# The order of the first loads and the place of the last copies in a gated linear attention with a mixture of attention experts

## Chip, cores and metric

The kernel runs on one core of a Trainium2 chip. The metric is the device time of one execution in microseconds (us), less is better. Three runs of the kernel before gave 327.18 us in the median (326.1 to 327.74).

## What is computed

Two stages. The first is a recurrence per batch and head with a decay rate for each row of the state; its output is the input of the second, attention with four experts, of which two are weighted per token.

```python
# q, k, v, alpha: (4, 8, 768, 48); alpha in 0.8 to 1
for t in range(S):
    state = alpha[:, :, t, :, None] * state + einsum('bhd,bhe->bhde', k[:, :, t], v[:, :, t])
    y[:, :, t] = einsum('bhd,bhde->bhe', q[:, :, t], state)
x = y.transpose(0, 2, 1, 3).reshape(B, S, 384)
logits = x @ w_gate                      # 4 experts, the best 2 weighted by softmax
for e in range(4):
    q, k, v = x @ wq[e], x @ wk[e], x @ wv[e]          # 64 wide
    a = softmax(causal(scale * q @ k.T))
    out += weight[e] * (a @ v @ wo[e])
```

## The kernel before

The recurrence is cut into 24 chunks of 128 steps (6 per batch). For each chunk VectorE makes running products of the decay rates with scans (`prep_r`, `prep_c`, line 181) and multiplies queries and keys by them (`prep_kq`, line 201). TensorE then transposes the keys (`gla_t`, line 237), forms the state's update (`gla_u`, line 266), the scores within the chunk (`gla_a`, line 220) and the output (`gla_y`, line 305). Three chunks are a unit; for each of the 8 units the attention with experts follows (projections, scores, softmax, transposes, products, and `outp`, line 499, into a result tile that is copied out of PSUM by `outp_o` and written by `store`). Products that need more than one rounded factor use a high and a low part; the low part of the value weights is made on TensorE by subtraction with a negated identity, `nid` (lines 730 and 731), after ScalarE has rounded the high part (line 747).

A planner in the kernel, run when the program is built, sets the order. Each step is an `op` with its dependencies, engines and an assumed length; `run` places them one by one. The opening is written by hand: `opening` (line 901) issues the first loads, calls `constants` (line 149) and then tells the planner with `came` when each load is taken to arrive. At most eight loads are outstanding: each load waits for the landing of the one eight places before it.

In the opening SyncE's queue issues chunk 0's first half of rates and of queries and keys, then rates and queries and keys of chunk 1, values of chunk 0, value weights, rates and queries and keys of chunk 2, and so on. Chunk 0 comes in two halves. Its second half is issued by ScalarE, after a table load, a small activation on `ones` (line 151) and the copy into `nid` (line 160). TensorE meanwhile runs warming matmuls on constants (line 896).

A range check on the scans ends in one integer, `cnt`. Every engine loads it into a register (`good`, line 960) and branches on it (line 967); if it is 0, the recurrence is computed again step by step. At the end of the last unit the third result tile is copied in two halves, by ScalarE and by VectorE, each stored on its own queue (lines 712 to 719); `good` depends on these two stores.

Of the kernel before, what the change touches and what calls it, by code (L numbers as in the profile page):

```python
# [12 lines left out]
AF = mybir.ActivationFunctionType  # L13
# [4 lines left out]
B, H, S, D = 4, 8, 768, 48  # L18
DM = H * D
# [4 lines left out]
NU = B * NC // HALF  # L24
NG = B * NC
NT = S // 128
P = 112
# [9 lines left out]
    P="t.0 u.0 a.0 wx.v.0 a.1 t.1 wx.v.1 y.0 u.1",  # L37
    V="r.0.0 c.0.0 r.0.1 c.0.1 kq.0.0 kq.0.1 r.1.0 c.1.0 kq.1.0 r.2.0 m.1.1 m.1.0 S.1 c.2.0 kq.2.0 xl.0 sa.1 kt.2 xl.1 kr.2 m.2.1 m.2.0 r.3.0 c.3.0",
    A="kr.0 kt.0 wvh m.0.1 m.0.0 wl.v.0 kt.1 kr.1 B.1 wl.v.1 wqh.0 xh.0 xh.1 B.2 vo.0.0 wqh.1 xh.2 kt.3 vo.0.1 ph.0.0.0 ph.0.0.1 woh ck.0 vo.0.2 ck.2 kr.3 B.3",
    G="e.0.0 e.0.1 e.1.0 m.0.1 m.0.0")  # L40
# [23 lines left out]
def tile_gla_moe(ctx: ExitStack, tc: tile.TileContext, qk_d, al_d, v_d, wqk_d, wv_d, wo_d, nat_d, vn_d, out_d):  # L64
    nc = tc.nc
    V, A, G, PE, SY = nc.vector, nc.scalar, nc.gpsimd, nc.tensor, nc.sync
# [5 lines left out]
    def fixed(name, shape, dt=F32):  # L72
        return consts.tile(shape, dt, name=name)
# [11 lines left out]
    def at(name):  # L85
        pool, i = where[name]
        return unit[pool][i]
# [4 lines left out]
    def view(x, *shape):  # L92
        n = "abcd"[:len(shape)]
        return x.rearrange(f"p ({' '.join(n)}) -> p {' '.join(n)}", **dict(zip(n[:-1], shape[:-1])))
# [5 lines left out]
    wo = view(raw[2][:, 780:780 + 2 * DM], 2, DM)  # L100
# [4 lines left out]
    def pieces(n):  # L105
        return [(0, 2), (2, 4)] if n == 0 else [(0, tiles(n))]
# [4 lines left out]
    def al(n, i=0):  # L111
        p0, p1 = pieces(n)[i]
        x = rates(n, i).rearrange("p (i z) -> p i z", i=2)
        return x[:, :, 0:(p1 - p0) * CW].rearrange("p i (a w) -> p i a w", w=CW)

    def load_al(n, i, eng):
        p0, p1 = pieces(n)[i]
        eng.dma_start(al(n, i), al_d[n, :, :, p0:p1])

    def load_q(n, i, eng):  # L120
        p0, p1 = pieces(n)[i]
        eng.dma_start(at(("T", n))[:, p0:p1, 0:2 * C], qk_d[n, :, p0:p1])

    def load_v(n):
        SY.dma_start(at(("v", n)).rearrange("s p e -> s (p e)"), v_d[n // NC, n % NC])
# [3 lines left out]
    ident = fixed("ident", [128, 128])  # L129
# [9 lines left out]
    ones = fixed("ones", [128, 1])  # L139
# [7 lines left out]
    nid = fixed("nid", [128, 128], F32R)  # L147

    def constants():
        G.memset(ones, 1.0)  # L150
        A.activation(ones, ones, AF.Copy)
        G.memset(d1r, TINY)
        G.memset(d1r[:, :, 0:1], 1.0)
        for t in d1c:
            V.memset(t, TINY)
        G.memset(mask, 1.0)
        G.affine_select(mask, mask, [[1, C]], OP.is_ge, 0.0, base=-(C - 1), channel_multiplier=1)
        G.memset(ident, 0.0)
        G.affine_select(ident, ident, [[1, 128]], OP.not_equal, 1.0, base=0, channel_multiplier=-1)
        A.activation(nid, ident, AF.Copy, scale=-1.0)  # L160
        for t in ST:
            G.memset(t, 0.0)
        for t in unit["kt"]:
            G.memset(t.rearrange("t p (s d) -> t p s d", s=2)[:, :, :, D:64], 0.0)
        G.memset(acc, 0.0)
        for t in SM:
            G.memset(t, 0.0)
        for t in [t for i, t in enumerate(unit["T"]) if i not in WHOLE]:
            for r in (32, 96):
                G.memset(t[r:r + 32, 3], 0.0)  # L170
        G.memset(cmask, 0.0)
        G.affine_select(cmask[:, 384:512], cmask[:, 384:512], [[-1, 128]], OP.is_ge, -1.0e30, base=0, channel_multiplier=1)
        G.memset(lm, 0.0)
        G.affine_select(lm, lm, [[1, NE], [-1, NE]], OP.is_gt, SMALL, base=0, channel_multiplier=0)
# [64 lines left out]
    def copy(eng, out, src):  # L239
        if eng == "A":  # L240
            A.activation(out, src, AF.Copy)  # L241
        else:
            V.tensor_copy(out, src)  # L243
# [255 lines left out]
                PE.matmul(po[:, 0:DM], y[:, h, 128 * i:128 * i + 128], w[:, pair, :], start=(m == 0), stop=(m == 5))  # L499
                m += 1  # L500

    def outp_o(eng, u, i, c0=0, c1=DM):
        copy(eng, at(("ot", u, i))[:, c0:c1], at(("po", u, i))[:, c0:c1])

    def store(eng, u, i, c0=0, c1=DM):
        t0 = 128 * (3 * (u % 2) + i)
        eng.dma_start(out_d[u // 2, t0:t0 + 128, c0:c1], at(("ot", u, i))[:, c0:c1])

    ops, users = [], {}
    KB = dict(La=396, Lq=393, Lv=262, cp=98, st=196)  # L510
# [1 line left out]
    def op(key, target, deps, alts, uses=(), take=(), mode="", land=0.0, lock=False):  # L512
        o = dict(key=key, target=target, deps=list(deps), alts=alts, uses=list(uses), take=list(take), mode=mode, land=land, lock=lock)
        ops.append(o)
        for n in o["uses"]:
            users[n] = users.get(n, 0) + 1
        return o

    def dv(n):
        return 0.15 + 0.00105 * n  # L520

    def da(n):
        return 0.19 + 0.00081 * n

    def either(f, n, *a):
        return [("A", da(n), lambda: f("A", *a)), ("V", dv(n), lambda: f("V", *a))]
# [178 lines left out]
    def out_ops(u):  # L705
        tail, seq, step, base = plan(u)
        for i in range(3):
            z = (base + step * 6 + OFF["w"] + 0.1 * i) * PACE
            op(("w", u, i), z, [("ol", u, 0, 0, 3), ("ol", u, 1, i, i + 1) if tail else ("ol", u, 1, 0, 3)],
               [("P", 1.06, lambda i=i: outp(u, i))], [("yy", u, 0), ("yy", u, 1)], [("po", u, i)], "f")  # L710
            po, ot = ("po", u, i), ("ot", u, i)
            if tail and i == 2:
                for x, E, Q in ((0, "A", A), (1, "V", SY)):
                    c = (192 * x, 192 * x + 192)
                    op(("wo", u, i, x), z, [("w", u, i)], [alt for alt in either(outp_o, 192, u, i, *c) if alt[0] == E], [po, ot],
                       [] if x else [ot])
                    op(("st", u, i, x), z, [("wo", u, i, x)], [("S" if x else "A", 0.4, lambda Q=Q, c=c: store(Q, u, i, *c))], [ot],
                       land=2.2)
                continue
            op(("wo", u, i), z, [("w", u, i)], either(outp_o, DM, u, i)[:1 if tail and i else 2], [po, ot], [ot])  # L720
            op(("st", u, i), z, [("wo", u, i)], [("S", 0.57, lambda i=i: store(SY, u, i))], [ot], land=2.2)

    def both(low, w, high):
        f = lambda E: E.tensor_tensor(low, w, high.bitcast(F32), OP.subtract)
# [176 lines left out]
    def opening():  # L901
        arrive, z = {}, [LEAD]

        def came(key, kb):
            z[0] += kb / RATE
            arrive[key] = (z[0], "S")

        for n in range(4):
            where["T", n] = ("T", n)
        for n in range(3):  # L910
            where["v", n] = ("v", n)
        where["al", 0] = ("at", 0)
        plain = list(range(UNITS["al"]))
        for n in range(1, 4):
            where["al", n] = ("a", (2 * n - 2, 2 * n - 1)) if n in WHOLE else ("al", plain.pop(0))
        where["at", "wqk"], where["at", "wvo"] = ("at", 1), ("at", 2)
        load_al(0, 0, SY)
        load_q(0, 0, SY)
        constants()
        load_al(0, 1, A)  # L920
        load_q(0, 1, A)
        for key, kb in (("La", 0, 0), 264), (("Lq", 0, 0), 262), (("La", 0, 1), 264), (("Lq", 0, 1), 262):
            came(key, kb)
        z[0] += 0.5
        for n in (1, 2):
            load_al(n, 0, SY)
            load_q(n, 0, SY)
            load_v(n - 1)
            came(("La", n, 0), 132 * tiles(n))
            came(("Lq", n, 0), 131 * tiles(n))  # L930
            came(("Lv", n - 1), 262)
            if n == 1:
                SY.dma_start(wv, wv_d)
                came(("Lw", 1), 400)
        SY.dma_start(wqk, wqk_d)
        came(("Lw", 0), 786)
        load_v(2)
        came(("Lv", 2), 262)
        load_al(3, 0, SY)
        load_q(3, 0, SY)  # L940
        came(("La", 3, 0), 396)
        came(("Lq", 3, 0), 393)
        SY.dma_start(wo, wo_d)
        came(("Lw", 2), 393)
        warm(7, 32)
        return arrive, z[0]

    okm = fixed("okm", [128, NG + 1])
    cnt = fixed("cnt", [1, 1], I32)
# [5 lines left out]
    z = (NG + 4) * PACE  # L955
# [1 line left out]
    op(("pk",), z, [("ok",)], [("P", 0.05, lambda: PE.matmul(at(("pk",))[0:1, 0:1], okm[:, 0:1], ones, start=True, stop=True))],  # L957
       [], [("pk",)], "f")
    op(("cnt",), z, [("pk",)], [("V", 0.15, lambda: V.tensor_scalar(cnt, at(("pk",))[0:1, 0:1], 128.0 * NG, None, op0=OP.is_ge))], [("pk",)])
    op(("good",), z, [("cnt",), ("st", NU - 1, 2, 0), ("st", NU - 1, 2, 1)], [("P", 0.05, lambda: good.append(nc.values_load(cnt, min_val=0, max_val=1)))])  # L960
    good = []

    with tc.manual_schedule():
# [3 lines left out]
    with tc.If(good[0] == 0):  # L967
# [7 lines left out]
        st, kv, tm = (unit["a"][i][:, 0:12 * D].rearrange("p (a d) -> p a d", a=12) for i in (2, 3, 4))  # L975
# [30 lines left out]
        for u in range(NU):  # L1006
# [3 lines left out]
            for i in range(3):  # L1010
                t0 = 128 * (3 * hf + i)
# [94 lines left out]
```

## Time and profile before

| | us |
|---|---|
| median of 3 runs | 327.18 (326.1 to 327.74) |
| profiled execution | 326.7 |
| its span (first to last instruction) | 325.0 |
| TensorE busy | 313.2 |
| VectorE busy | 249.3 |
| ScalarE busy | 208.9 |
| GpSimd busy | 128.5 |
| mean granted clock of TensorE, as a share of full | 0.984 |

The profile shows one execution. Times in it count from the span's first instruction. PE is TensorE, DVE VectorE, ACT ScalarE, POOL GpSimd, SP SyncE; a q behind a name is the engine's sequencer, where DMAs are issued, registers loaded and branches taken. In the timeline a row gives start, length, engine, line, operation, output and input, count, and in brackets how long the engine had been idle and what ended that.

### The profile page before, as it was taken

To read this page: it belongs to the slowest core of one execution; us is meant where nothing else is said; L and a number is where in the kernel's file an instruction comes from. 1 tells how busy PE (TensorE), PEld (TensorE's weight loads), DVE (VectorE), ACT (ScalarE), POOL (GpSimd) and SP (SyncE) were. 2 spreads that over 40 slices of the span, in tenths; PEclk is the share of its full clock that TensorE was granted. 3 is DMA by queue.
4 is the path that set the end of the run, shared out by engine and by line. 5 is a ranking of instruction groups with operands and counts; after the bars stand their busy time and mean duration, and the time that the engine had idled before them with its cause. 6 is when DMAs were issued, how large, how long until landed. Compare 5 with 4: busy or idle time off the path is not lost.

```text
span 325.0 us, 11059 instructions
## 1 busy us (share of the span) xinstructions
PE 313.2 (96%) x4416; PEld 267.7 (82%) x4416; DVE 249.3 (77%) x679; ACT 208.9 (64%) x588; POOL 128.5 (40%) x197
## 2 busy tenths in 40 slices
PE   7299999999999999999999999999999999999995
PEld 2178998988997997998997997898897997888693
DVE  3569988999899998999799998766875745487620
ACT  2136598778776784757957775656873766377841
POOL 6014514553546257507507037405171344023510
PEclk9579999999999999999999999999999999999999
DMA  7993437464253335624352524302200000102001
GB/s 207 391 359 115 108 84 256 137 183 133 78 169 93 113 92 151 174 93 141 91 189 76 151 63 131 98 35 84 87 4 2 0 5 16 59 1 75 2 29 59
DMA packets 27037, 35.21 MB, mean 108 GB/s; under 512 B 2304, under 2 KB 23008, under 8 KB 26976
## 3 DMA queue, kind: packets, MB, share of 16 engines
q1 hardware_dynamic: 26288, 33.78, 34.1%
q8 instruction: 37, 0.61, 0.8%
q10 hardware_dynamic: 688, 0.62, 0.6%
q14 instruction: 24, 0.20, 0.2%
HBM read 27.61 MB, written 4.72 MB: 99 GB/s over the span
## 4 chain that ended last, share of the span: by engine, by line
PE 94%; DMA 3%; issue 1%; ACT 0%; POOL 0%; POOLq 0%
PE g L328 16%; PE g L455 12%; PE g L480 12%; PE g L305 11%; PE g L403 11%; PE g L354 8%; PE g L499 8%; PE g L220 7%; PE g L896 4%; DMA at<-in_al_dram 3%; PE g L237 2%; PE g L266 2%; PE g L730 0%; ACT ms L228 0%; PE g L731 0%
## 5 line engine op out<-in xcount | busy, mean ns | idle before, releaser
L440 POOL TENSOR_SCALAR a<-a,cf,gw 128x128 f32<-128x128 f32 (+5 forms) x96 | 81.7, 864 | 71.1 <-DVE cf L434 45.3
L428 ACT ACTIVATE a<-a,mx 128x256 f32<-128x256 f32 (+3 forms) x96 | 51.6, 540 | 8.9 <-DVE mx L417 8.8
L455 PE MATMUL g<-ident,a 128*128 128x128 f32 x336 | 53.8, 277 | 0.0
L328 PE MATMUL g<-x,wqkh 128*128 128x384 f32 x192 | 51.7, 350 | 0.0
L455 PEld LDWEIGHTS g<-ident,a 128*128 128x128 f32 x336 | 39.7, 140 | 5.8 <-issue 2.3
L232 POOL TENSOR_SCALAR_AFFINE_SELECT ms<-ms 128x512 f32<-128x512 f32 x31 | 21.3, 700 | 57.9 <-ACT ms L228 56.0
L243 DVE COPY at<-g 128x512 f32<-128x512 f32 (+3 forms) x62 | 29.2, 480 | 16.8 <-PE g L455 15.8
L480 PE MATMUL g<-at,vg 128*32 128x384 f32 (+2 forms) x648 | 39.7, 389 | 0.0
L403 PE MATMUL g<-k,q 64*128 64x256 f32 (+3 forms) x384 | 39.2, 336 | 0.0
L241 ACT ACTIVATE at<-g 128x512 f32<-128x512 f32 (+3 forms) x66 | 30.4, 466 | 8.3 <-PE g L455 6.5
L480 PEld LDWEIGHTS g<-at,vg 128*32 128x32 f32 x648 | 19.2, 110 | 18.6 <-issue 15.3
L305 PE MATMUL g<-ms,v 128*32 128x128 f32 x768 | 33.1, 274 | 0.0
L328 PEld LDWEIGHTS g<-x,wqkh 128*128 128x128 f32 x192 | 33.0, 189 | 0.0
L403 PEld LDWEIGHTS g<-k,q 64*128 64x128 f32 x384 | 28.6, 185 | 5.2 <-issue 2.3
L328 PE MATMUL g<-x,wqkl 128*128 128x384 f32 x96 | 32.3, 337 | 0.0
L354 PE MATMUL g<-wvh,x 128*128 128x260 f32 x144 | 31.7, 296 | 0.0
L417 DVE CUSTOM_DVE_ANT_0 a<-g,cmask 128x128 f32<-128x128 f32 (+2 forms) x64 | 28.2, 483 | 2.0 <-PE g L403 1.8
L499 PE MATMUL g<-woh,yy 128*128 128x384 f32 x96 | 28.1, 351 | 0.0
L220 PE MATMUL g<-T 48*128 48x128 f32 x384 | 26.4, 280 | 0.0
L220 PEld LDWEIGHTS g<-T 48*128 48x128 f32 x384 | 24.7, 193 | 1.4 <-issue 0.7
L228 ACT ACTIVATE ms<-g 128x512 f32<-128x512 f32 x31 | 17.3, 592 | 11.4 <-PE g L220 11.3
L354 PEld LDWEIGHTS g<-wvh,x 128*128 128x128 f32 x144 | 24.0, 190 | 0.4 <-ACT ms L228 0.4
(113 smaller groups left out, 629.1 us busy)
## 6 DMA issues: line engine op xcount, KB each, us to landing
al<-in_al_dram SPq DMA_DIRECT2D x21, 387.0 KB, 4.0
T<-in_qk_dram SPq DMA_DIRECT2D x21, 384.0 KB, 4.1
v<-in_v_dram SPq DMA_DIRECT2D x24, 256.0 KB, 4.1
out_dram<-ot SPq DMA_DIRECT2D x23, 192.0 KB, 2.3
T<-T SPq DMA_DIRECT2D x42, 48.2 KB, 2.2
a<-in_al_dram SPq DMA_DIRECT2D x2, 516.0 KB, 6.8
T<-in_qk_dram SPq DMA_DIRECT2D x2, 512.0 KB, 7.7
at<-in_wqk_dram SPq DMA_DIRECT2D x1, 768.0 KB, 8.6
```

The lines of the kernel that those rows point to most:

```text
L220: PE.matmul(pa[s][:, C * p:C * p + C], t[r:r + D, p, C:2 * C], t[r:r + D, p, 0:C], start=True, stop=True, tile_position=(r, 0))
L241: A.activation(out, src, AF.Copy)
L243: V.tensor_copy(out, src)
L305: PE.matmul(o[32 * j:32 * j + 32, k], l, r, start=(i == 0), stop=(i == len(parts) - 1), tile_position=(0, 32 * j))
L328: PE.matmul(pj[:, :W3], w[:, kt, cs], x[:, kt, :], start=(i == 0), stop=(i == 8))
L354: PE.matmul(pv[:, 0:260], x[:, kt, 128 * i:128 * i + 128], w[:, kt, :], start=(m == 0), stop=(m == 8))
L403: PE.matmul(sc(u, pair, i, e, x, c1 - c0), q[r, i0, ts], k[r, i1, c0:c1], start=(y == 0), stop=(y == 2), tile_position=(64 * e, 0))
L428: A.activation(a[:, c0:c1], src, AF.Exp, bias=mx[:, 1:2], scale=-1.0 if last else 1.0, accum_out=sm[:, x:x + 1])
L440: G.tensor_scalar(a[:, 0:n], a[:, 0:n], CF[u % 2][:, 3 * pair + i, e:e + 1], gw[:, u, i, eg:eg + 1], op0=OP.mult, op1=OP.mult)
L455: PE.transpose(pt[:, 128 * (j - j0):128 * (j - j0) + 128], a[:, 128 * j:128 * j + 128], ident)
L480: PE.matmul(o[r:r + 32, lo:n1], v[:, j % 3, 64 * eg + x:64 * eg + x + 32], at(("at", u, pair, e))[:, min(j, 4), at_off(j) + lo:at_off(j) + ...
L499: PE.matmul(po[:, 0:DM], y[:, h, 128 * i:128 * i + 128], w[:, pair, :], start=(m == 0), stop=(m == 5))
```

## The change

Chunk 0's two halves of rates go out first, both on SyncE's queue. Its two halves of queries and keys go out on ScalarE's queue, right behind the activation on `ones`. The copy into `nid` comes after them. The planner is told the new order of arrival and 0.2 us less for it. At the end, `good` no longer depends on the last stores but on the last product, and the copies of the last two result tiles depend on `good`; the last tile is copied whole by ScalarE and stored on its queue.

```diff
     def constants():
-        G.memset(ones, 1.0)
-        A.activation(ones, ones, AF.Copy)
         G.memset(d1r, TINY)
...
-        A.activation(nid, ident, AF.Copy, scale=-1.0)
...
-            if tail and i == 2:
-                for x, E, Q in ((0, "A", A), (1, "V", SY)):
-                    c = (192 * x, 192 * x + 192)
...
-            op(("wo", u, i), z, [("w", u, i)], either(outp_o, DM, u, i)[:1 if tail and i else 2], [po, ot], [ot])
-            op(("st", u, i), z, [("wo", u, i)], [("S", 0.57, lambda i=i: store(SY, u, i))], [ot], land=2.2)
+            late = tail and i > 0
+            op(("wo", u, i), z, [("w", u, i)] + [("good",)] * late, either(outp_o, DM, u, i)[:1 if late else 2], [po, ot], [ot])
+            op(("st", u, i), z, [("wo", u, i)], [("A", 0.4, lambda i=i: store(A, u, i)) if tail and i == 2 else
+                                                ("S", 0.57, lambda i=i: store(SY, u, i))], [ot], land=2.2)
...
-        load_al(0, 0, SY)
-        load_q(0, 0, SY)
+        for i in (0, 1):
+            load_al(0, i, SY)
+        G.memset(ones, 1.0)
+        A.activation(ones, ones, AF.Copy)
+        for i in (0, 1):
+            load_q(0, i, A)
         constants()
-        load_al(0, 1, A)
-        load_q(0, 1, A)
-        for key, kb in (("La", 0, 0), 264), (("Lq", 0, 0), 262), (("La", 0, 1), 264), (("Lq", 0, 1), 262):
+        A.activation(nid, ident, AF.Copy, scale=-1.0)
+        for key, kb in (("La", 0, 0), 264), (("La", 0, 1), 264), (("Lq", 0, 0), 262), (("Lq", 0, 1), 262):
             came(key, kb)
-        z[0] += 0.5
+        z[0] += 0.3
...
-    op(("good",), z, [("cnt",), ("st", NU - 1, 2, 0), ("st", NU - 1, 2, 1)], [("P", 0.05, lambda: good.append(nc.values_load(cnt, min_val=0, max_val=1)))])
+    op(("good",), z, [("cnt",), ("w", NU - 1, 2)], [("P", 0.05, lambda: good.append(nc.values_load(cnt, min_val=0, max_val=1)))])
```

Between these places the order of the instructions is the same on all five engines. The opening on ScalarE before (`at_63` holds the rates of chunk 0, `T_85` its queries and keys; `kt` are transposed keys):

```order
L151 ACT_TABLE_LOAD
L151 ACTIVATE ones<-ones 128x1
L160 ACTIVATE nid<-ident 128x128
L118 DMA at_63<-in_al_dram 128x2x258
L122 DMA T_85<-in_qk_dram 128x2x256
L241 ACTIVATE kt_69<-g_101 128x3x2x16
L241 ACTIVATE kt_69<-g_101 128x6x48
```

and now:

```order
L911 ACT_TABLE_LOAD
L911 ACTIVATE ones<-ones 128x1
L122 DMA T_85<-in_qk_dram 128x2x256 x2
L915 ACTIVATE nid<-ident 128x128
L238 ACTIVATE kt_69<-g_101 128x3x2x16
L238 ACTIVATE kt_69<-g_101 128x6x48
```

Both loads of queries and keys now stand ahead of the copy into `nid`, and the rates are gone from this queue. The opening on SyncE's queue now (`a` and `T_86` are rates, and queries and keys, of chunk 1, `v_92` values of chunk 0, `at_65` the value weights; the second `a` and `T_87` belong to chunk 2):

```order
L118 DMA at_63<-in_al_dram 128x2x258 x2
L118 DMA a<-in_al_dram 128x2x516
L122 DMA T_86<-in_qk_dram 128x4x256
L125 DMA v_92<-in_v_dram 128x512
L927 DMA at_65<-in_wvg_dram 128x780
L118 DMA a<-in_al_dram 128x2x516
L122 DMA T_87<-in_qk_dram 128x4x256
L125 DMA v_93<-in_v_dram 128x512
```

Before, the second place held `T_85<-in_qk_dram 128x2x256`; the rest is as it was. The end on ScalarE before (`ot` are result tiles, `yy` the products' operands):

```order
L486 ACTIVATE yy_81<-g_108 128x128
L486 ACTIVATE yy_81<-g_102 128x128
L241 ACTIVATE ot_96<-g_107 128x384
L241 ACTIVATE ot_97<-g_104 128x192
L507 DMA out_dram<-ot_97 128x192
L960 TENSOR_LOAD cnt
L967 COMPARE_AND_BRANCH
```

and now:

```order
L483 ACTIVATE yy_81<-g_108 128x128
L483 ACTIVATE yy_81<-g_102 128x128
L954 TENSOR_LOAD cnt
L238 ACTIVATE ot_96<-g_107 128x384
L238 ACTIVATE ot_97<-g_104 128x384
L504 DMA out_dram<-ot_97 128x384
L961 COMPARE_AND_BRANCH
```

The answer's load stands ahead of the last two copies, and the branch directly behind the last store. On SyncE the load likewise stands ahead of its last store, which is now that of `ot_96`.

## Rows read from the trace of the kernel before

**Rows 1.** The page: shares of the chain that ended last.
```profile
PE 94%; DMA 3%; issue 1%; ACT 0%; POOL 0%; POOLq 0%
```

**Rows 2.** Timeline of ScalarE, 0 to 32.
```profile
2.10 0.20 ACT L151 ACTIVATE ones<-ones 128x1 f32<-128x1 f32 x1
...
4.09 0.64 ACTq L118 DMA_DIRECT2D at<-in_al_dram  x1
4.77 0.86 ACTq L122 DMA_DIRECT2D T<-in_qk_dram  x1
```

**Rows 3.** Timeline of SyncE's queue, 0 to 32.
```profile
3.48 0.62 SPq L125 DMA_DIRECT2D v<-in_v_dram  x1
4.14 0.43 SPq L933 DMA_DIRECT2D at<-in_wvg_dram  x1
4.61 0.69 SPq L118 DMA_DIRECT2D a<-in_al_dram  x1
```

**Rows 4.** DMA issues, 0 to 9: count, KB each, us from issue to landing.
```profile
at<-in_wvg_dram SPq DMA_DIRECT2D x1, 390.0 KB, 6.9
T<-in_qk_dram ACTq DMA_DIRECT2D x1, 256.0 KB, 9.0
v<-in_v_dram SPq DMA_DIRECT2D x1, 256.0 KB, 6.1
a<-in_al_dram SPq DMA_DIRECT2D x1, 516.0 KB, 8.5
```

**Rows 5.** DMA queues, 7 to 8, then 9.5 to 10: packets, MB; q1 SyncE's, q10 ScalarE's.
```profile
q1 hardware_dynamic: 339, 0.37, 108.3%
...
q1 hardware_dynamic: 54, 0.13, 68.2%
q10 hardware_dynamic: 54, 0.06, 32.2%
```

**Rows 6.** Timeline of VectorE, 0 to 32.
```profile
12.06 0.70 DVE L181 TENSOR_TENSOR_SCAN at<-at,d1r 128x258 f32<-128x258 f32 x1 [6.26 <-DMA at<-in_al_dram]
...
13.60 1.27 DVE L201 TENSOR_TENSOR T<-T,at 128x512 f32<-128x512 f32 x2
...
18.67 1.23 DVE L181 TENSOR_TENSOR_SCAN a<-a,d1r 128x516 f32<-128x516 f32 x1
...
22.63 1.29 DVE L224 TENSOR_TENSOR ms<-g,mask 128x512 f32<-128x512 f32 x2 [2.51 <-PE g L220]
```

**Rows 7.** Timeline of TensorE at 14, and the chain's piece at 21.
```profile
14.37 1.03 PE L237 MATMUL g<-ident,T 128*128 128x128 f32 x3 [6.83 <-issue]
...
21.39 1.09 PE g L220 x16
```

**Rows 8.** Two stretches: busy time of five engines, granted clock, DMA share, GB/s.
```profile
8.00:10.00 2.00, 0.00 (x0) 0.00 (x0) 0.00 (x0) 0.00 (x0) 0.00 (x0) 0.89 1.05 400
18.00:20.00 2.00, 2.00 (x33) 1.82 (x24) 1.97 (x3) 0.00 (x0) 0.00 (x0) 0.55 1.08 387
```

**Rows 9.** The end: timelines of ScalarE and SyncE, then lines 960 and 967.
```profile
317.31 0.49 ACT L241 ACTIVATE ot<-g 128x384 f32<-128x384 f32 x1 [1.22 <-PE g L499]
318.37 0.33 ACT L241 ACTIVATE ot<-g 128x192 f32<-128x192 f32 x1 [0.56 <-PE g L499]
...
317.83 1.62 SPq L507 DMA_DIRECT2D out_dram<-ot  x2
...
L960 ACTq TENSOR_LOAD <-cnt x1: 487/487/487, 319.1 to 319.1; - x1
...
L967 SPq EVENT_SEMAPHORE  x8: 17/17/17, 323.0 to 323.6; - x8
...
L967 ACTq COMPARE_BRANCH  x1: 62/62/62, 319.7 to 319.7; - x1
L967 SPq COMPARE_BRANCH  x1: 50/50/50, 320.4 to 320.4; - x1
...
L967 ACTq EVENT_SEMAPHORE  x1: 17/17/17, 322.4 to 322.4; - x1
```

## What the change does to the time, from these rows

> **What bounds the kernel now.** The first view is the chain that ended last: TensorE holds 94% of it [rows 1]. The order of its instructions is fixed, so whatever lets it begin its first real work earlier moves everything behind it, as long as nothing else is late on the way. Two stretches are not TensorE's: the opening and the end.
>
> The second view is the opening, engine by engine. ScalarE finishes its table load and its little activation at 2.30, but the DMA of chunk 0's second half of rates goes out at 4.09 and that of its queries and keys at 4.77 [rows 2]. These queries and keys land 9.0 us after their issue, at 13.8 [rows 2, 4]. The rates of that half are what VectorE waits 6.26 us for, until 12.06; its two products of chunk 0 run from 13.60 to 14.87 [rows 6]. TensorE, out of its warming matmuls at 7.54, starts the transposes of chunk 0 at 14.37 after 6.83 us of nothing [rows 7]. Its granted clock went to the lower of its two levels (1.2 instead of 2.4 GHz) on the way: 0.89 is the mean of 8 to 10, so it fell at about 9.56, two us after the last matmul, and with a mean of 0.55 over 18 to 20 it came back at 19.8 [rows 8]. So 4.4 us of TensorE's work behind the transposes (15.40 to 19.8) ran at half speed.
>
> The third view is the end. After TensorE's last product, two copies of half a tile run one after the other, each with its store on another queue; then SyncE reads the answer of the range check, branches at 320.4, and its first instruction behind the branch runs at 323.0. ScalarE branches at 319.7 and goes on at 322.4 [rows 9].
>
> **What the change does to the opening.** On SyncE's queue the second half of the rates takes the place of the first half of the queries and keys, same size within 2 KB; the queue issues as many loads ahead of chunk 1 as before. So that half should land where the replaced load did, before 5.8, when VectorE's first half ends: VectorE was idle for 6.26 us up to 12.06, from 5.80 on [rows 6]. A half (scan, reciprocal, scan) takes 13.60 - 12.06 = 1.54, so both halves are scanned by 7.34 and the 6.26 us wait is gone.
>
> Next in line are the queries and keys, now both on ScalarE's queue, with no wait ahead of them, from 2.3 to about 3.8 (0.64 and 0.86 each [rows 2]). The second one decides. No row shows a load on this queue so early, so I bound it. *Early*: it has landed by 7.34 and costs nothing. *Late*: as slow as the same load was before, 9.0 us from its issue at 3.0, so 12.0. Between them I go by bytes, since loads issued one after another landed in that order. The value load of chunk 0 was the last of 258 + 256 + 516 + 512 + 256 = 1,798 KB and landed at 3.48 + 6.1 = 9.6 [rows 3, 4]. Ahead of and with the second queries load there will be 258 x 2 + 516 + 256 + 512 + 256 = 2,056 KB. But the two queues share packet by packet once both have work: 54 packets of each in half a us [rows 5]. Its 256 rows of 1 KB are then through when half of the 512 KB of SyncE's neighbour is: 1,800 KB, **9.6**. I take that; without the sharing it is 256 KB later, 0.7 us by the 375 GB/s of 7 to 8 (0.37 MB [rows 5]), 10.3.
>
> What speaks against more: before, ScalarE's transfers, issued at 4.09, had moved nothing by 8.0; between 7 and 8 only SyncE's queue shows packets [rows 5]. A second queue did not pass what had been issued ahead of it.
>
> The Trainium skill says as much of this edit (DMA: Bandwidth & Descriptors, "Issuing engines are not separate DMA queues"): loads issued by several engines run on the same DMA engines, and a second issuer saves issue time alone. By that rule the second load lands at 10.3 and the sum below is 0.7 us smaller, 320.1; rows 5 agree with it up to 8 us and not on the sharing after that.
>
> From 9.6 VectorE needs half of 1.27 us, so the products end at 10.2 instead of 14.87: VectorE is **4.6 us** earlier. TensorE's transposes ended 0.53 us behind (15.40), and from there to the end of the scores of chunk 1 (21.39 + 1.09 = 22.48) its chain ran 7.08 us without a wait [rows 7]. At the old clock it ends at 10.8 + 7.1 = 17.9, 4.6 earlier. At the full clock the 4.4 us shrink to 2.2, and it ends near 15.6, 6.9 earlier. Which? TensorE still stops at 7.54, now for some 2.7 us with two transposes in between, not for 6.8. The clock fell after two us of rest, so it may fall, but it comes back sooner. I take the middle, **5.8 us**.
>
> What covers this, and how thinly: VectorE begins the rates of chunk 2 at 18.67 - 4.6 = 14.1. They landed at 4.61 + 8.5 = 13.1 [rows 3, 4] and have the same bytes ahead of them now; 1.4 us later VectorE can take the masks it took at 22.63 [rows 6], so it caps the gain at about 7.1. The value weights landed at 4.14 + 6.9 = 11.0 and now have 514 KB more ahead, so about 12.4; ScalarE's rounding and TensorE's difference of them come at 13.5 to 14. If they land a us later, TensorE loses that us. The identity's negated copy moves behind two issues, to about 4; its first user, the subtraction of the rounded value weights, comes no sooner than 13. Weights, values and rates behind these have ten us and more of slack. From there on the order on all engines is the same, and all wait for each other, so the gain should last to the end.
>
> **What it does to the end.** The answer waits for nothing late and is read ahead of the last two copies. On ScalarE this takes 0.487 us [rows 9] in a pause of over 1 us before the copy at 317.31: hidden; uncovered it would cost 0.5. The last tile is one copy of 0.49 where the first half took 0.33, so 0.16 more, then its store, then the branch without the read: 319.7 + 0.16 - 0.49 = 319.4 less 0.1 for what lay between, and with the same 2.7 us to the next instruction 322.0 instead of 322.4. SyncE's last store is the one at 317.83 [rows 9]; its branch moves to about 318.5 and its next instruction to 321.1, with eight waits of 0.6 us for landings. What is late next is ScalarE at 322.0, where SyncE was done at 323.6: **1.5 us** less (between 0.9, if a landing is late, and 1.9). TensorE's warming matmuls at the end shrink from four long ones to a short one and are not waited for.
>
> **Sum.** The profiled execution took 326.7 (span 325.0 and 1.7 around it), 0.5 below the median 327.18 of the three runs. 326.7 - 5.8 - 1.5 = **319.4**.
>
> **Rivals.**
> *The queues share from the start.* The Trainium skill states (same page, "Queues, rings and completion order") that each DMA engine goes round between the queues that have work. As a mechanism here: the queries go half and half with SyncE's loads from about 4.5 on and land by 7.4. TensorE then follows the value weights (12.4 + 0.9 + about 1.4 = 14.7 for the end of chunk 1's scores) and gains 7.8: 317.4. For it: equal packets in rows 5. Against: nothing moved until 8. Chance 0.17.
> *ScalarE's load is as slow as before.* It lands at 12.0 and the clock falls: 4.6 - 2.4 = 2.2 in the opening, 323.0; with 10.3 and the low clock 3.9, 321.3. For it: the 9.0 us row. Against: eight loads had been issued ahead of it then, five now. Chance 0.2 for 320.8 to 323.2.
> *The opening's gain is given back.* The DMA engines run without pause up to 24 us and the bytes do not change; a later load that TensorE now reaches early would take it back. Each has ten us of slack. 1.5 from the end and 1 or so remain: 324.2. Chance 0.06.
> *The clock stays down.* If TensorE, now waiting for data in short pauses from 8 to 20, were kept at 1.2 GHz, each two us at that level would cost one. Place: the stretch from 10 us on. It decides once the low level lasts 15 us longer than before (to about 35): 7.3 is then gone; at 18 us longer 9 is gone and the time is 328.4. The Trainium skill has the low level as the default that activity lifts (TensorE: Matmul & The Clock Gate, "The HAM clock gate"). Rows 7 and 8 speak against it: one unbroken stretch from 14.37 lifted it at 19.8. Chance 0.02.
> *The queries wait behind all of SyncE's loads* and land as late as before: the end's 1.5 alone, 325.2 to 326. Chance 0.03.
>
> **Numbers.** Forecast 0.52. The range runs from 317.0 (first rival, with 0.4 for run scatter) to 322.8 (most of the second); the first rival is in, of the second a small part is out, of the last three all: about 0.15 to 0.2 is outside. A measurement of this kernel tells about 0.5% (1.6 us) from no change. All cases but the last three, and most of the third, are faster by more: 0.93; within: 0.05; slower: 0.02.
>
> **What would show it.** Right: VectorE's scans of chunk 0 back to back from 4.2 to 7.3; the second queries load landing between 8.5 and 10.3; TensorE's transposes of chunk 0 ending by 10.8 and the scores of chunk 1 between 15.5 and 18; SyncE's instruction behind the branch 2 to 4 us before the end, with ScalarE's the last one. Wrong: that load at 12 or later, a granted clock of 0.5 past 17, a wait of TensorE for the value weights or of VectorE for chunk 2's rates of over one us, or a gain at 25 us that is gone at 300.

## The result and the profile after

| | us | ratio to the kernel before, 95% interval |
|---|---|---|
| kernel before, 4 runs beside it | 327.24 (326.1 to 327.74) | |
| changed kernel, 4 runs | 318.61 (318.09 to 318.76) | 0.9738 (0.971 to 0.9766) |
| forecast | 319.4 (317.0 to 322.8) | |

The profiled execution took 318.76 with a span of 317.0, 8.0 less than the span before. Sign and size came out as forecast, 0.8 below it. But the parts of the sum did not: the opening gave 8.0 where 5.8 stood, the end 0.4 where 1.5 stood, and 0.4 was lost on the way. And the opening's gain has another cause than the one given.

**The opening.** ScalarE's timeline after, to be laid beside [rows 2] (start, length, engine, line, operation, output and input):

```profile
0.80 1.28 ACT L911 ACT_TABLE_LOAD   x1 [0.80 <-PEq L1094]
0.94 0.98 ACTq L122 DMA_DIRECT2D T<-in_qk_dram  x2
2.10 0.20 ACT L911 ACTIVATE ones<-ones 128x1 f32<-128x1 f32 x1
```

Both loads of queries and keys go out from 0.94 on, while the table load still runs and before the activation that stands ahead of them in the program. The prediction had them at 2.3 and 3.0.

The DMA queues after, 2 to 3, then 3 to 4, then 4 to 5 (packets, MB; q10 is ScalarE's, q1 SyncE's):

```profile
q10 hardware_dynamic: 218, 0.22, 66.0%
q1 hardware_dynamic: 5, 0.01, 2.0%
...
q1 hardware_dynamic: 237, 0.24, 80.2%
q10 hardware_dynamic: 66, 0.06, 25.6%
...
q10 hardware_dynamic: 255, 0.25, 71.8%
q1 hardware_dynamic: 89, 0.08, 29.1%
```

The first load of queries and keys moves ahead of SyncE's loads, the second mostly behind them; they land 2.7 and 4.1 us after their issue, the later one at 5.55. The rates pay a little: the first half lands at 4.64 instead of 4.06, the second at 6.2, just before VectorE takes it at 6.33.

VectorE's timeline after, against [rows 6]:

```profile
4.74 0.70 DVE L178 TENSOR_TENSOR_SCAN at<-at,d1r 128x258 f32<-128x258 f32 x1 [2.73 <-DMA at<-in_al_dram]
...
7.84 1.27 DVE L198 TENSOR_TENSOR T<-T,at 128x512 f32<-128x512 f32 x2
...
14.72 1.29 DVE L221 TENSOR_TENSOR ms<-g,mask 128x512 f32<-128x512 f32 x2
```

The wait of 6.26 us is gone, both halves are scanned in one run, and the products end at 9.1 instead of 14.87: 5.75 earlier, bound by the scans once the first half of the rates has landed, and no longer by ScalarE's loads.

TensorE's timeline, a piece of the chain, and two windows, against [rows 7, 8]:

```profile
8.61 0.88 PE L234 MATMUL g<-ident,T 128*128 128x128 f32 x3 [0.61 <-issue]
9.33 1.25 PE L887 MATMUL g<-d1r 128*128 128x512 f32 x4
...
10.97 1.16 PE L217 MATMUL g<-T 48*128 48x128 f32 x16
```

```profile
13.39 1.09 PE g L217 x16
```

```profile
8.00:10.00 2.00, 1.25 (x6) 0.75 (x6) 2.00 (x3) 0.47 (x2) 0.00 (x0) 1.00 1.06 391
18.00:20.00 2.00, 2.00 (x44) 1.64 (x34) 1.82 (x5) 1.27 (x3) 1.18 (x2) 1.00 1.05 387
```

TensorE rests 0.61 us where it rested 6.83, and its granted clock stays at the upper level. The scores of chunk 1 end at 14.48 instead of 22.48, **8.0** earlier. This is one execution of each kernel: in the four other profiled kernels with the same loads (`e1`, `e3`, `changed_again` and `e3_again` below) the scores end between 14.6 and 15.3, so the opening gives 7.2 to 8.0.

**The body.** The 8.0 holds to about 48 us. Then one scan of VectorE takes 1.36 us, where the same one took 0.95 before, and TensorE waits 0.41 at 63.7:

```profile
48.91 1.36 DVE L178 TENSOR_TENSOR_SCAN al<-al,d1r 128x387 f32<-128x387 f32 x1
```

```profile
63.72 0.55 PE L234 MATMUL g<-ident,T 128*128 128x128 f32 x3 [0.41 <-ACT ms L225]
```

From there on the shift is 7.6: the last product ends at 310.7 instead of 318.3. In `changed_again`, the same program, this scan takes 0.95, the opening gives 7.6, and 7.4 are left at the last product. So it is not shown that the loss of 0.4 belongs to the change.

**The end.** From there to the end of the span it is 6.33, before 6.69: only 0.36 less. The two lines of the branch and of what follows it (duration in ns, then first and last start in us), against [rows 9]:

```profile
L961 PEldq COMPARE_BRANCH  x1: 4082/4082/4082, 309.5 to 309.5; - x1
...
L961 ACTq COMPARE_BRANCH  x1: 54/54/54, 311.7 to 311.7; - x1
...
L961 PEldq EVENT_SEMAPHORE  x1: 51/51/51, 313.6 to 313.6; - x1
L961 ACTq EVENT_SEMAPHORE  x1: 17/17/17, 314.3 to 314.3; - x1
```

```profile
L1096 PEldq DRAIN  x2: 8/8/8, 313.8 to 316.8; - x2
...
L1096 ACTq EVENT_SEMAPHORE  x2: 17/17/17, 314.8 to 317.0; - x2
...
L1096 PEldq EVENT_SEMAPHORE  x2: 51/51/51, 316.6 to 317.0; - x2
```

ScalarE goes on 2.6 us behind its branch, as forecast, and reaches the first of the last two events at 314.8, like SyncE and VectorE. TensorE drains at 313.8 and then takes until 316.6. The other engines wait 1.9 us for it. In the kernel before SyncE drained only at 324.2, and all of them, TensorE included, stood at that event together, at 324.4:

```profile
L1102 SPq DRAIN  x3: 7/7/13, 324.2 to 324.5; - x3
...
L1102 PEldq EVENT_SEMAPHORE  x2: 51/51/51, 324.4 to 324.9; - x2
```

### The profile page after: what moved, and what is told of

The parts are those of the page before. It is cut to its first block, busy times and chain, and to the rows that moved or that the text cites. A ratio compares the mean times of both kernels' runs of the same rounds, so it can differ in the third digit from the quotient of the medians.

```text
span 317.0 us, 11044 instructions
## 1 busy us (share of the span) xinstructions
PE 308.2 (97%) x4410; PEld 265.4 (84%) x4410; DVE 249.5 (79%) x678; ACT 208.9 (66%) x588; POOL 128.2 (40%) x197
## 4 chain that ended last, share of the span: by engine, by line
PE 95%; DMA 1%; DVE 1%; ACT 0%; issue 0%; ACTq 0%; DVEq 0%
PE g L325 16%; PE g L452 13%; PE g L477 12%; PE g L302 11%; PE g L400 11%; PE g L351 8%; PE g L496 8%; PE g L217 7%; PE g L887 3%; PE g L263 2%; PE g L234 2%; DMA at<-in_al_dram 1%; DVE at L178 1%; PE g L721 0%; DVE T L198 0%
## 5 line engine op out<-in xcount | busy, mean ns | idle before, releaser
L437 POOL TENSOR_SCALAR a<-a,cf,gw 128x128 f32<-128x128 f32 (+5 forms) x96 | 80.5, 851 | 71.4 <-DVE cf L431 45.5
L229 POOL TENSOR_SCALAR_AFFINE_SELECT ms<-ms 128x512 f32<-128x512 f32 x31 | 22.1, 724 | 56.2 <-ACT ms L225 56.2
L477 PEld LDWEIGHTS g<-at,vg 128*32 128x32 f32 x648 | 19.3, 109 | 18.5 <-issue 15.3
L217 PE MATMUL g<-T 48*128 48x128 f32 x384 | 25.7, 275 | 0.0
L217 PEld LDWEIGHTS g<-T 48*128 48x128 f32 x384 | 24.0, 187 | 1.3 <-DVE T L198 0.4
L302 PE MATMUL g<-T,S 112*32 112x128 f32 x480 | 24.2, 272 | 0.0
```

The lines of the kernel that those rows point to most:

```text
L217: PE.matmul(pa[s][:, C * p:C * p + C], t[r:r + D, p, C:2 * C], t[r:r + D, p, 0:C], start=True, stop=True, tile_position=(r, 0))
L302: PE.matmul(o[32 * j:32 * j + 32, k], l, r, start=(i == 0), stop=(i == len(parts) - 1), tile_position=(0, 32 * j))
L437: G.tensor_scalar(a[:, 0:n], a[:, 0:n], CF[u % 2][:, 3 * pair + i, e:e + 1], gw[:, u, i, eg:eg + 1], op0=OP.mult, op1=OP.mult)
L477: PE.matmul(o[r:r + 32, lo:n1], v[:, j % 3, 64 * eg + x:64 * eg + x + 32], at(("at", u, pair, e))[:, min(j, 4), at_off(j) + lo:at_off(j) + ...
```

## The experiments

### Which part carries the gain

`e1_opening_alone`: the opening's part of the change on the kernel before.

```diff
     def constants():
-        G.memset(ones, 1.0)
-        A.activation(ones, ones, AF.Copy)
...
-        A.activation(nid, ident, AF.Copy, scale=-1.0)
...
-        load_al(0, 0, SY)
-        load_q(0, 0, SY)
+        for i in (0, 1):
+            load_al(0, i, SY)
+        G.memset(ones, 1.0)
+        A.activation(ones, ones, AF.Copy)
+        for i in (0, 1):
+            load_q(0, i, A)
         constants()
-        load_al(0, 1, A)
-        load_q(0, 1, A)
+        A.activation(nid, ident, AF.Copy, scale=-1.0)
...
```

> The new opening with the old end. Theory (the opening carries nearly all): scores of chunk 1 end near 14.5 as in the changed kernel, 8.0 us before the kernel before; some 0.4 is lost further on; the end takes the 6.7 us from the last product to the span's end that it took before. Time 7.4 to 7.8 below the kernel before, 319.0 to 319.8. Rival (the two parts share the gain, 5.8 and the rest at the end, as predicted): 5.8 below, 321.4.

319.68, ratio 0.9754 (0.9724 to 0.9784). The last product ends at 310.6.

`e2_end_alone`: the end's part on the kernel before.

```diff
...
-            if tail and i == 2:
...
+            late = tail and i > 0
...
-    op(("good",), z, [("cnt",), ("st", NU - 1, 2, 0), ("st", NU - 1, 2, 1)], ...
+    op(("good",), z, [("cnt",), ("w", NU - 1, 2)], ...
```

> The old opening with the new end. Theory (behind the branch, TensorE's sequencer stands still a second time and is the last engine): the end takes about 6.3 us from the last product, 0.3 to 0.5 less than before: 326.7 to 326.9 against 327.2. Rival (ScalarE is the last engine and the end is worth 1.5): 325.7.

326.63, ratio 0.997 (0.9942 to 0.9999). From the last product to the end of the span (the tail, from here on) it is 6.45 (6.69 before), with TensorE's event again last by 1.8 us. So the opening is worth over 7 us. The end is worth little: its tail is 0.24 shorter, and the interval of the ratio allows 0 to 1.9 us. The two ratios add up to 2.8% where the whole change has 2.6%; neither part needs the other.

### What in the opening carries it

Three runs move ScalarE's two loads in time, a fourth puts them on the other queue.

`e5_queries_after_identity`: the changed kernel with both loads behind `constants()` and the copy into `nid`.

```diff
-        for i in (0, 1):
-            load_q(0, i, A)
         constants()
         A.activation(nid, ident, AF.Copy, scale=-1.0)
+        for i in (0, 1):
+            load_q(0, i, A)
```

> The changed kernel with both loads of queries and keys moved behind the copy into nid, so that they go out at about 2.9 and 3.6 instead of 0.94 and 1.45. Theory A (the early issue, beside the table load, is what brought them so soon): the first half's rates land at 4.1 again, the second queries load lands between 8 and 10, the two products of chunk 0 end at 8.7 to 10.5 instead of 9.1, and the time is 0 to 1.5 us above the changed kernel. Rival B (the second queue shares from the start at any issue time): the queries land by 7.3, the products start at 7.2, and the time is 0 to 0.6 us below the changed kernel. Rival C (as slow as the 9.0 us load of the kernel before): landing at 12, the time 2.5 to 3.5 us above.

326.82, ratio 0.9974 (0.9944 to 1.0003): 8 us above the changed kernel, more than any of the three allowed. With the rates still first and alone on SyncE's queue, the whole gain is gone. The chain's first pieces, VectorE, TensorE and a window of this run:

```profile
1.58 3.16 DMA at<-in_al_dram
4.74 0.02 issue
4.76 9.34 DMA T<-in_qk_dram
```

```profile
6.58 0.70 DVE L178 TENSOR_TENSOR_SCAN at<-at,d1c 128x258 f32<-128x258 f32 x1
12.12 0.69 DVE L198 TENSOR_TENSOR T<-T,at 128x512 f32<-128x512 f32 x1 [4.83 <-DMA T<-in_qk_dram]
14.20 0.69 DVE L198 TENSOR_TENSOR T<-T,at 128x512 f32<-128x512 f32 x1 [1.39 <-DMA T<-in_qk_dram]
```

```profile
15.21 2.34 PE L887 MATMUL g<-d1r 128*128 128x512 f32 x4
```

```profile
14.00:16.00 2.00, 1.05 (x2) 0.61 (x3) 1.80 (x2) 0.55 (x3) 0.00 (x0) 0.50 1.08 401
```

VectorE has scanned all rates by 7.28 and then waits 4.83 for queries. The scores of chunk 1 end at 22.48, the very time of the kernel before. The second load goes out at 4.76, 0.02 behind the landing of the second half of the *rates*, which it does not use. Why, the program's own waits tell. ScalarE's loads of the kernel before, of this run and of the changed kernel, each with the semaphore it waits for (the eight of the loads are DMAHW0 to DMAHW7, used in turn):

```
before   L118 DMA at_63<-in_al_dram 128x2x258 [waits DMAHW0_49]
before   L122 DMA T_85<-in_qk_dram 128x2x256 [waits DMAHW1_49]
e5       L122 DMA T_85<-in_qk_dram 128x2x256 [waits DMAHW0_49]
e5       L122 DMA T_85<-in_qk_dram 128x2x256 [waits DMAHW1_49]
after    L122 DMA T_85<-in_qk_dram 128x2x256 x2
```

At most eight loads are outstanding, and ScalarE's two were ninth and tenth in the order: SyncE's eight had been counted ahead of them. In the kernel before, too, they waited for the landing of SyncE's first two loads. Its chain shows it:

```profile
0.81 3.25 DMA at<-in_al_dram
4.06 0.02 issue
4.09 7.95 DMA at<-in_al_dram
```

The change moves the two loads ahead of `nid`, where they are among the first eight and wait for nothing; now the ninth and tenth are SyncE's loads for chunk 2, which have time.

`e10_identity_first`: the copy into `nid` stays ahead of the loads, but GpSimd writes the identity first, so that the copy is done sooner.

```diff
     def constants():
-        G.memset(d1r, TINY)
-        G.memset(d1r[:, :, 0:1], 1.0)
...
-        G.memset(ident, 0.0)
-        G.affine_select(ident, ident, [[1, 128]], OP.not_equal, 1.0, base=0, channel_multiplier=-1)
...
+        G.memset(d1r, TINY)
+        G.memset(d1r[:, :, 0:1], 1.0)
+        G.memset(ident, 0.0)
+        G.affine_select(ident, ident, [[1, 128]], OP.not_equal, 1.0, base=0, channel_multiplier=-1)
+        A.activation(nid, ident, AF.Copy, scale=-1.0)
         for i in (0, 1):
             load_q(0, i, A)
         constants()
-        A.activation(nid, ident, AF.Copy, scale=-1.0)
```

> The changed kernel with the copy into nid ahead of the two loads of queries and keys, and with GpSimd writing the identity first, so that the copy does not wait for it and the loads go out between 0.94 and 4.0, at 2.4 to 3.5 by my guess. Theory (the landing hangs on how much SyncE has issued by then, and the two queues share what comes after): the second of them lands at 8.5 to 10.5, the products end at 9.5 to 11.5, and the time is 319 to 322.5. Rival (the queue of ScalarE starts moving only about 4 to 5 us after its issue whatever was issued on the other): landing at 6.5 to 8, the time as the changed kernel. Second rival (a late second queue lands 8.7 us behind its issue, as in the run before): landing at 11.5 to 13, the time 323 to 326.

325.39, ratio 0.9971 (0.9935 to 1.0008), the time of the second rival. Its chain has the same handover:

```profile
1.57 3.65 DMA at<-in_al_dram
5.22 0.02 issue
5.24 7.05 DMA T<-in_qk_dram
```

One of the two loads is now among the eight: it goes out at 2.08 and lands 5.5 us later, at 7.6. The other is tenth (SyncE's queries and keys of chunk 2 are ninth), waits for the second half of the rates, goes out at 5.24 and lands at 12.3. The scores of chunk 1 end at 20.0. So the expectation's idea of an issue at 2.4 to 3.5 was wrong for the second load, and its time followed the later one. The first load, behind the copy but inside the count, was in time: VectorE's first product starts at 7.60, against 7.84 in the changed kernel.

`e8_only_early_issue`: the kernel before with ScalarE's two loads (rates and queries of the second half) ahead of `constants()`, nothing else.

```diff
     def constants():
-        G.memset(ones, 1.0)
-        A.activation(ones, ones, AF.Copy)
...
         load_al(0, 0, SY)
         load_q(0, 0, SY)
+        G.memset(ones, 1.0)
+        A.activation(ones, ones, AF.Copy)
+        load_al(0, 1, A)
+        load_q(0, 1, A)
         constants()
-        load_al(0, 1, A)
-        load_q(0, 1, A)
```

> The kernel before with one step moved: ScalarE's two loads of chunk 0 go out behind the activation on ones instead of behind the copy into nid. The order of rates and queries on SyncE and the end stay as they were. Theory (all of the opening's gain comes from ScalarE's loads going out at 0.9 instead of 4.1, none from the rates being first): VectorE's first scan at 4.0 to 4.8, its products of chunk 0 at 7.2 to 8.2, the scores of chunk 1 end at 14.0 to 14.8, and the time is 319 to 320, as with the new opening alone (319.7). Rival (the rates have to be ahead of the queries on one queue): VectorE waits at least 1 us for the second half's rates, the products end past 10, and the time is 321 to 324.

319.34, ratio 0.9771 (0.9748 to 0.9793): the theory's time, and that of the whole new opening. VectorE and the chain:

```profile
4.50 0.70 DVE L179 TENSOR_TENSOR_SCAN at<-at,d1r 128x258 f32<-128x258 f32 x1 [2.48 <-POOL T L168]
...
7.57 1.27 DVE L199 TENSOR_TENSOR T<-T,at 128x512 f32<-128x512 f32 x2
```

```profile
13.48 1.09 PE g L218 x16
```

The scores of chunk 1 end at 14.57, against 14.48 in the changed kernel. **The rates' being first is worth nothing; the early issue is worth all of it.** The move does two things: the loads no longer stand behind the copy, and they no longer wait for a landing. No run leaves them behind the copy as it was and takes only the wait away; the first load of `e10` comes nearest to that, and it was in time.

`e4_queries_on_sync`: the changed kernel with all four loads on SyncE's queue.

```diff
-            load_q(0, i, A)
+            load_q(0, i, SY)
```

> The changed opening, but the two loads of queries and keys follow the two of rates on SyncE's queue. Theory (the queues share one stream of transfers in the order of issue, and the second queue is worth the time of its issues): the first rates land at 4.1 instead of 4.6, both queries by 6.7, the products begin at 7.3 instead of 7.84, but all later loads are issued 1.2 us later; chunk 1's rates land at 8.5 and decide nothing, chunk 2's at 13 to 13.7 and cost VectorE up to 0.5. Time 318.0 to 319.2, the same as the changed kernel. Rival (the second queue is what brought the gain): 2 us slower, 320.6.

319.72, ratio 0.9783 (0.9734 to 0.9832), between theory and rival, and 0.8 above the changed kernel on this chip (`changed_again`, 318.9). The products come even sooner, at 7.23, but four issues in a row push the values of chunk 0 back, and the chain goes by them:

```profile
4.61 6.74 DMA v<-in_v_dram
...
14.37 1.09 PE g L217 x16
```

They go out at 4.61 (3.52 in the changed kernel), and the scores of chunk 1 end at 15.46: 1.0 later than in the first profile of the changed kernel, 0.6 later than in `changed_again`. So the second queue is worth at most about 1 us here, and what it saves is the time that two issues take, 1.1 us for the values. The Trainium skill says so (DMA: Bandwidth & Descriptors, "Issuing engines are not separate DMA queues"): a second issuer saves only the time of issuing. This run agrees with it, with these 1.1 us.

### The clock

`e6_less_warming`: the opening's call for four long warming matmuls (the profile counts each twice) asks for one, so that TensorE rests 5.27 us ahead of its transposes instead of 0.61.

```diff
-        warm(7, 32)
+        warm(7, 8)
```

> The changed kernel with 8 instead of 32 warming columns in the eight matmuls' last argument, so that TensorE ends its warming some 5 us earlier and rests about 5 us ahead of its transposes. Theory (the 2.2 us that the gain in the opening was larger than forecast came from a clock that did not fall): the granted clock falls to 0.5 near 8 to 9, the scores of chunk 1 end 1 to 2.5 us later, and the time is 1 to 2.5 us above the changed kernel. Rival (the opening waits for data anyway): the clock falls but the time is the same within 0.4.

319.41, ratio 0.9752 (0.9693 to 0.9811); the changed kernel beside it (`changed_again`) took 318.9, 0.9743 (0.9686 to 0.98).

> The changed kernel once more, on the chip of the next three. All theories: 318.6 within 0.5, TensorE's last product about 7.6 us earlier than in the kernel before.

The whole time, 0.5 longer, lies just above the rival's 0.4 and below the theory's 1 to 2.5; the trace shows the loss that the theory asked for, but not the fall of the granted clock. TensorE's timeline of this run, and a window:

```profile
9.75 2.34 PE L887 MATMUL g<-d1r 128*128 128x512 f32 x4
...
12.81 1.77 PE L217 MATMUL g<-T 48*128 48x128 f32 x16
```

```profile
10.00:12.00 2.00, 2.00 (x4) 0.76 (x3) 1.93 (x3) 1.40 (x3) 0.19 (x1) 1.00 1.04 381
```

The group of four takes 2.34 instead of 1.25, exactly what it took in `e5` at a granted clock of 0.50. Here the column says 1.00 all the same: the trace has no clock record for this stretch, and the column counts it as full. So at the start of a program the durations have to be read, not the column. By them the clock did not fall in the rest but had not risen before it: the last warming matmul ahead of the rest takes 1.06 us, as one of that group does, against 0.59 in the changed kernel. The scores of chunk 1 end at 16.92, 2.4 later than in the changed kernel; 0.3 of it is a later start of the transposes, **2.1** the clock. The last product ends at 313.5, 2.6 later than in `changed_again`. The profiled span is only 1.0 longer (the medians 0.5), because the tail is 1.5 shorter, 4.59: the program is a few instructions shorter, and TensorE's late event is gone. The next runs are about that.

### TensorE's late event at the end

`e3_moved_target`: sixteen small matmuls are added to the part that the branch skips. They never run, but they move the branch's target in the program.

```diff
         V.memset(st, 0.0)
+        for x in range(16):
+            warm(0, 8)
```

> The changed kernel with sixteen more warming matmuls on TensorE inside the part that is skipped; nothing more is executed, but the code behind the branch lies elsewhere. Theory (the 2.9 us in which TensorE's sequencer stands still behind the branch, 313.8 to 316.65, are the loading of more code, since its code starts near the end of what the branch loads): they go, the other engines' 314.8 decides, and the time falls by 1.5 to 1.9 to 316.7 to 317.1. Rival (TensorE waits there for a signal or for its matmuls to drain): no change, 318.6.

317.49, ratio 0.9683 (0.966 to 0.9707). The time is 0.4 above the theory's 316.7 to 317.1 and well below the rival's 318.6. From the last product to the end it is 4.74 instead of 6.33, and TensorE's event comes with ScalarE's:

```profile
L1098 ACTq EVENT_SEMAPHORE  x2: 17/17/17, 315.2 to 315.7; - x2
...
L1098 PEldq EVENT_SEMAPHORE  x2: 51/51/51, 315.2 to 315.7; - x2
```

What is shown is that the place of TensorE's instructions decides about 1.6 us at the end, although none of the added ones is executed. All profiled kernels with the new end bear it out: the tail is 6.1 to 6.5 in the six that leave TensorE's instructions where they were (the changed kernel, `changed_again`, `e2`, `e4`, `e5`, `e10`) and 4.6 to 4.7 in the four that move them (this run, `e3_again`, `e9`, `e6`).

The traces also show what TensorE may be waiting for. A DMA queue of the kind `instruction`, q8, moves one packet of 16 KB that begins 1.0 to 1.6 us behind the start of TensorE's branch, and a second one later. The queues from 314 to 315 (packets, MB), in the changed kernel and in this run:

```profile
q8 instruction: 1, 0.02, 7.0%
...
q8 instruction: 1, 0.02, 7.5%
```

In the changed kernel the second packet is through at 315.42 and TensorE's event follows at 316.65, 1.2 us behind; in the six it is 1.2 to 1.5. In this run the packet is through at 315.92 and the event, at 315.19, did not wait for it; nor did it in the other three. So in the slow cases TensorE seems to wait for this second load of code; that it does is inferred from the order of these times. The Trainium skill states (Runtime: NRT & Kernel Launch, "Instruction fetch mechanics") that a taken branch whose target is not among the blocks held must fetch the target's block before execution goes on. The first packet behind the branch agrees with it; on the second the page says nothing.

`e7_before_moved_target`: the same sixteen matmuls in the kernel before.

> The kernel before with sixteen warming matmuls added to the part that the branch skips, which moves the branch's target as in the earlier run of the changed kernel that gained 1.1 us by it. Theory (in the kernel before, SyncE's late branch hides TensorE's second wait for code): the time is the same within 0.5, and the last events of TensorE and SyncE stay together. Rival (TensorE's code sets the end of the kernel before too): 1 to 1.6 us faster than the kernel before.

327.28, ratio 1.0007 (0.9968 to 1.0046), as the theory had it. In the kernel before SyncE's late branch sets the end (SyncE drains at 324.2 in both), and TensorE's place in the program costs nothing.

`e3_again` and `e9_halves_and_target`, on one chip. The second has the moved target and the halves split over the queues, rates ahead of queries on each:

```diff
-        for i in (0, 1):
-            load_al(0, i, SY)
+        load_al(0, 0, SY)
+        load_q(0, 0, SY)
...
-        for i in (0, 1):
-            load_q(0, i, A)
+        load_al(0, 1, A)
+        load_q(0, 1, A)
```

> The changed kernel with the moved target once more, for the comparison with the next on the same chip: 317.5 within 0.5.

> The moved target, and in the opening the first half of chunk 0 (rates, then queries) on SyncE's queue and the second half on ScalarE's, both at once from 0.8. Theory: the first half's rates land sooner than 4.6, so VectorE starts at 4.1 to 4.5 and TensorE's transposes 0.2 to 0.5 sooner; the time is 317.0 to 317.6, 0 to 0.5 below the moved target alone. Rival (what the first loads gain, the values of chunk 0 and the value weights take back, as with all four loads on SyncE): 317.5 to 318.5.

317.5, ratio 0.9709 (0.9686 to 0.9732), and 317.34, ratio 0.9701 (0.9678 to 0.9725). The two can't be told apart: in `e9` the products come 0.3 sooner than in the changed kernel, then TensorE waits 0.78 for the values of chunk 0. Both are 1.1 to 1.6 us below the medians of the changed kernel (318.61 and 318.9).

## Why the prediction was right, and where it was not

**Right**: the opening is where the time goes, the order behind it is fixed, so the gain lasts; the wait of 6.26 us vanishes and nothing of over a us takes its place; the move of the `nid` copy and the read of the answer ahead of the copies cost nothing; range and sign.

**Wrong, the reason for the opening's gain.** The step "the queries and keys, both on ScalarE's queue, with no wait ahead of them, from 2.3" put the late issue of [rows 2] down to the work ahead of the loads on ScalarE. What set it was the wait for a place among eight outstanding loads: 4.09 follows the landing of SyncE's first load at 4.06, and 4.77 that of the second. The text ahead of the prediction names this limit; the prediction did not count these two loads against it. Ahead of the copy, and among the first eight, they go out at 0.94, beside the table load. The landing at 9.6, the base of the 4.6 us, fell with it: it was 5.55. So did the cap of 7.1: VectorE takes the masks 7.9 earlier, at 14.72. The half of the rates that "should land where the replaced load did, before 5.8" landed later than that (at 6.2; the replaced load at 4.77), and it cost nothing, because VectorE took it at 6.33; that the rates go first did not matter either (`e8`). The prediction's account of late loads holds: `e5`, issued at 4.0 and 4.8, lands after 8 to 9 us, and nothing of it moved before 8, as in [rows 5].

**The rival "queues share from the start"** came closest for the opening: 7.8 us, measured 8.0. But the queries did not go half and half with SyncE's loads from 4.5 on; the two queues took turns from 2 on, with 218 packets to 5, then 66 to 237, then 255 to 89.

**Mis-sized, the clock.** "I take the middle" (1.2 of 2.2 us). TensorE rested only 0.61 us and the clock did not fall; `e6` puts what the lower level costs in this stretch at 2.1. With VectorE's 5.75 that makes 7.9 of the 8.0.

**Wrong, the end.** "What is late next is ScalarE at 322.0: 1.5 us less." ScalarE came as forecast, TensorE 1.9 us later; the prediction looked at ScalarE and SyncE, and set TensorE aside for its warming matmuls. Without TensorE's delay the tail is 1.6 shorter still: 1.95 below the kernel before's (`e3`), where 1.5 (0.9 to 1.9) had been reckoned.

**Not foreseen, 0.4 us** given back at 49 us in the profiled execution. Opening 8.0, less 0.4, plus 0.4 at the end: 8.0 of the span. The forecast's 7.3 was near it because the errors in opening and end had opposite signs. That the time came so close is luck.

## What to carry to other kernels

When a DMA is issued late, look at what landed 0.02 us before it went out: a limit on outstanding transfers makes a load wait for one that it has nothing to do with, and here its place in the count, not its queue, decided. Put the loads that the first work needs among the first that are counted, and let those with slack be the ones that wait. Once a late engine is off the end, list the last events of *all* engines, the one with the most work included, before the gain is booked.

## What was not expected of the hardware

- A DMA on ScalarE's queue goes out at 0.94 while ScalarE's table load runs from 0.80 to 2.08 and an activation ahead of it in program order starts only at 2.10.
- Being issued later costs more than the delay: the second load of queries landed 4.1 us behind an issue at 1.44, 7.05 behind one at 5.24 and 9.34 behind one at 4.76, where both queries loads were late.
- Sixteen instructions that never run took 1.1 us off the time of one kernel and changed nothing in another.
- The same scan of 128x387 took between 0.95 and 1.36 us in these runs, with GpSimd busy beside it both times. What stretches it stays open.
